# Gated layer, first chunk: SyncE issues the load of the next set's raw blocks ahead of the store of the current set's summed blocks

## The chip, the cores and the metric

The kernel runs on one core of one Trainium2 chip. The metric is the time of one execution on the device in microseconds (us); lower is better. Times of runs and times inside the profile are given apart, because the profile's span leaves out a little at both ends.

## The reference, cut to what matters

Three layers follow one another: windowed attention, a mixture of experts (one expert for each token), and a gated layer. The change is in the gated layer alone:

```python
def _moe2_ref(x, w_gate, w_val, w_out):
    gate = 1.0 / (1.0 + np.exp(-(x @ w_gate)))
    val = x @ w_val
    return (gate * val @ w_out).astype(np.float32)
```

Here x has 3072 tokens of 512 numbers, w_gate and w_val are 512 x 1536, w_out is 1536 x 512, all in float32.

## The kernel before, in words

The gated layer (class `Gated`) cuts the tokens into four chunks of 768 (`NCH` = 4, `CT` = 768). For each chunk there are two phases. The first phase computes gate and value products; it walks over twelve sets (`NSET` = 12). An even set holds a 256-column piece of w_gate and the odd set after it the same piece of w_val. The products are made with the seven-product scheme for two-by-two blocks (Strassen-Winograd): a set has four raw weight blocks and four sums of them, and seven of these eight blocks enter one product each. Every factor is split into a high and a low part, so that one product is six matmuls (two halves of 128 rows, three combinations, `product`, line 1329); a set is 42 matmuls. The second phase multiplies with w_out (`second`, line 1425).

What has to be there before a set can be multiplied, in the first chunk:

- `afetch(s)` (line 1254 in the first chunk) loads the four raw blocks of set s, 512 KB, from DRAM into a buffer named `raw`. That pool has two buffers, taken in turn, so set s+2 goes where set s was, and its load waits until all readers of set s are done.
- `asum(s)` makes the four sums with four GpSimd instructions (line 1265) into the same buffer. In its last line (1266) SyncE is told to store blocks 1 to 7, 896 KB, to the DRAM tensor `us[s]`. The three later chunks load the finished blocks from there (line 1259) and make no sums.
- `asplit(s, z)`, z = 0 and 1, turns four and then three blocks into high parts (ScalarE, line 1277) and low parts (VectorE, line 1278). These go to the tile `set`, of which there are two as well.

`first(s)` is the body of one set, written as a generator. Its order is: `asum(s+2)` in the first chunk; products X and Y; `asplit(s+1, 0)`; product Z; `asplit(s+1, 1)`; `afetch(s+3)`; now and then a load or a split of w_out blocks (`ofetch`, line 1282, at sets 3, 5, 8 and 10, 768 KB; `osplit`, lines 1287 to 1289, at sets 6 and 8, whose low part GpSimd makes and whose 1536 KB SyncE stores to `wz`); then products W, X, Z, W again, with VectorE additions between them (lines 1352, 1362, 1381, 1392, 1397, 1401). A product that uses the same accumulator a second time waits until VectorE has read the first. In odd sets GpSimd multiplies gate and value (line 1385).

The order is written out by hand. Each engine runs its own instructions strictly in that order, and so does SyncE, on which all of these loads and stores lie in one queue: a store that waits for the sums holds up the load written behind it. In program order SyncE has, for the body of set r: store of set r+2, load of set r+3, then the w_out transfers. The sets 0 to 2 are prepared in `lead(f)`, during the last eight steps of the mixture of experts: `afetch(0)` and `asum(0)` at step 4, `afetch(1)` and `asum(1)` at step 6, `afetch(2)` and the start of `first(0)` at step 7. The buffers of sets 0 and 1 are before that used by two loads of the layer's input (`yfetch`, line 1231), whose last reader is VectorE, line 1247. The input's stores `yT` come from line 1129.

Of the kernel before, what the change touches and what calls it, by code (L numbers as in the profile page):

```python
# [57 lines left out]
NSET = 2 * NJ  # L58
# [168 lines left out]
def graph():  # L227
# [12 lines left out]
    for t in range(NTILE):  # L240
# [15 lines left out]
        for s in (2 * t, 2 * t + 1):  # L256
# [4 lines left out]
            for j in range(4):  # L261
                first = [("NS", WIN if t else 128, s % 2)] if t < 2 and j == 0 else []
                add(
                    ("TTR", s, j), [("QK", s)] + first, [("QK", s, j - 2)] if j >= 2 else (),
                    cost=0.318 if i else 0.21,
                )
                add(
                    ("EXP", s, j), [("TTR", s, j)] + ([("PT", s - 3, 1)] if s >= 3 and j == 0 else []),
                    cost=0.38 if i else 0.293,
                )  # L270
# [937 lines left out]
class Gated:  # L1208
# [53 lines left out]
    def asum(self, s):  # L1262
        x = self.raw[s]
        for o, a, b, op in ((4, 0, 1, ALU.add), (6, 2, 0, ALU.subtract), (5, 4, 2, ALU.subtract), (7, 3, 5, ALU.subtract)):
            self.tc.nc.gpsimd.tensor_tensor(x[:, o, :], x[:, a, :], x[:, b, :], op=op)  # L1265
        self.tc.nc.sync.dma_start(out=self.g.us[s], in_=x[:, 1:, :].rearrange("p b n -> p (b n)"))

    def halves(self):
        return self.set_p.tile([128, 2, NJ * CH], FR, tag="set", name="set2")
# [65 lines left out]
    def first(self, s):  # L1335

        nc = self.tc.nc
        j, m = divmod(s % NSET, 2)
        V, A, G = nc.vector, nc.scalar, nc.gpsimd
        last = s % NSET == NSET - 1  # L1340
        X, Y, Z, W = (self.psum(b, f"q{b}")[:, :CH] for b in ((2, 3, 0, 1) if m else (6, 7, 4, 5)))
        u2 = self.tm.tile([128, CH], F32, tag="u2", name="u2", bufs=2)
        c, r = divmod(s, NSET)
        more = c + 1 < NCH
        if c == 0 and r < NSET - 2:
            self.asum(s + 2)
        if more and r >= NSET - 2:
            self.ysum(c + 1, r - NSET + 2)
        self.product(X, 1, 0, s)
        A.activation(u2, X, AF.Copy)  # L1350
        self.product(Y, 4, 4, s)
        V.tensor_tensor(u2, Y, u2, op=ALU.add)  # L1352
        yield
        if last:
            self.hsplit(0, 0, 2)
        else:
            self.asplit(s + 1, 0)
        self.product(Z, 5, 5, s)
        at = lambda half, tok: self.h[:, 2 * j + half, tok * CH : tok * CH + CH]
        dst = (lambda half, tok: self.g.op.tile([128, CH], F32, tag="t", name="t", bufs=3)) if m else at  # L1360
        d22 = dst(1, 1)
        V.tensor_tensor(d22, Z, u2, op=ALU.add)
        if last:
            self.hsplit(0, 2, 4)
        else:
            self.asplit(s + 1, 1)
        if r < NSET - 3:
            self.afetch(s + 3)
        elif more and r < NSET - 1:
            self.yfetch(c + 1, r - NSET + 3)  # L1370
        if c == 0:
            if r in (3, 5):
                self.ofetch((r - 3) // 2)
            if r in (6, 8):
                self.osplit((r - 6) // 2, G)
            if r in (8, 10):
                self.ofetch((r - 8) // 2 + 2)
        elif r in (2, 4, 6):
            self.oload(c, r // 2 - 1)
        self.product(W, 3, 3, s)  # L1380
        V.tensor_tensor(d22, W, d22, op=ALU.add)  # L1381

        def gate(d, half, tok):
            if m:
                (V if last else G).tensor_tensor(at(half, tok), at(half, tok), d, op=ALU.mult)  # L1385
            else:
                A.activation(d, d, AF.Sigmoid)

        gate(d22, 1, 1)
        self.product(X, 2, 1, s, False)  # L1390
        if m:
            V.tensor_tensor(at(0, 0), X, at(0, 0), op=ALU.mult)  # L1392
        else:
            A.activation(at(0, 0), X, AF.Sigmoid)
        self.product(Z, 0, 6, s, False)
        d21 = dst(1, 0)
        V.tensor_tensor(d21, Z, u2, op=ALU.add)
        gate(d21, 1, 0)
        self.product(W, 6, 2, s, False)
        d12 = dst(0, 1)  # L1400
        V.tensor_tensor(d12, W, u2, op=ALU.add)  # L1401
        gate(d12, 0, 1)
        yield
# [76 lines left out]
    def lead(self, f):  # L1480

        if f < 2:
            self.yfetch(0, f)
        if f in (1, 2):
            self.ysum(0, f - 1)
        if 2 <= f < 6:
            self.ysplit(0, f // 2 - 1, f % 2)
        if f == 3:
            sg = self.tm.tile([128, 1], F32, name="sg")
            self.tc.nc.scalar.activation(sg, self.g.nval[:, 0:1], AF.Sigmoid)  # L1490
        if f in (4, 6):
            self.afetch(f // 2 - 2)
            self.asum(f // 2 - 2)
        if f == 7:
            self.afetch(2)
            self.now = self.first(0)
            next(self.now)

# [435 lines left out]
```

## Time and profile before

| what | value |
|---|---|
| three runs | 1129.24, 1132.36, 1136.51 us; median 1132.36 us |
| the profiled execution's own time | 1134.08 us |
| its span, first to last instruction | 1132.2 us |
| mean granted TensorE clock | 0.965 of full speed |
| TensorE matmul busy | 1039.4 us, 92% of the span |
| VectorE, ScalarE, GpSimd busy | 832.5, 566.4 and 437.5 us |
| first chunk's first phase | about 545.3 to 668.5 us of the span |

How to read it: TensorE is busy nearly all the time, but matmuls are stretched when the granted clock is at its lower level, so the busy share alone doesn't show what a stage loses. A stage is read by comparing it with a stage that does the same multiplications under other conditions. Times "at 617.37" are microseconds from the start of the span.

### The profile page before, as it was taken

Reading aid. Unit: us, or ns where it says so; the run is one execution under the profiler, and the core shown is the slowest. Engines: PE = TensorE matmul, PEld = TensorE weight load, DVE = VectorE, ACT = ScalarE, POOL = GpSimd, SP = SyncE. Lnnn points to the kernel's source line nnn. Section 1 sums busy time; section 2 is a strip of 40 time slices with the busy share of each in tenths; the row PEclk is TensorE's granted clock in tenths of the full one; section 3 lists DMA queues with packets and bytes.
Section 4 is the critical chain, followed back from the end, with each engine's and each line's share of the span. In section 5 each row is a group of like instructions: output and inputs, shape, how many; then the busy total and the mean of one; then the engine's idle time right before and its main releaser. Section 6 shows DMA issues by size and latency. Waiting matters only on the chain. (4 is left out here: it accounts for less than half of the span.)

```text
span 1132.2 us, 21478 instructions
## 1 busy us (share of the span) xinstructions
PE 1039.4 (92%) x7983; PEld 990.5 (87%) x7983; DVE 832.5 (74%) x1663; ACT 566.4 (50%) x1027; POOL 437.5 (39%) x612
## 2 busy tenths in 40 slices
PE   7887878689999999999888798999999999999995
PEld 5776767679889999999777798999999999999995
DVE  6887769756678888885545689766896669866783
ACT  7997869533344445455424346344453445444440
POOL 7898778830221221213546660411503242222102
PEclk9999889798999999999989899999999999999998
DMA  9999996386698889976355658764365644656051
GB/s 188 198 179 166 187 159 146 118 189 223 200 282 274 288 281 334 305 237 192 115 179 182 246 189 299 259 235 184 110 236 190 228 167 139 247 197 243 33 213 70
DMA packets 176216, 229.45 MB, mean 203 GB/s; under 512 B 90243, under 2 KB 140038, under 8 KB 172518
## 3 DMA queue, kind: packets, MB, share of 16 engines
q1 hardware_dynamic: 170566, 214.04, 63.4%
q0 software_dynamic: 5008, 13.93, 3.5%
q8 instruction: 65, 1.06, 0.4%
q14 instruction: 49, 0.40, 0.2%
q10 hardware_dynamic: 528, 0.02, 0.0%
HBM read 163.13 MB, written 60.51 MB: 198 GB/s over the span
## 5 line engine op out<-in xcount | busy, mean ns | idle before, releaser
L1329 PE MATMUL q<-yo,set 128*128 128x384 f32 x2016 | 364.8, 342 | 20.0 <-DVE t L1381 5.9
L1329 PEld LDWEIGHTS q<-yo,set 128*128 128x128 f32 x2016 | 356.7, 192 | 27.1 <-DVE t L1381 7.5
L1425 PE MATMUL p<-wy,set 128*128 128x256 f32 x1458 | 176.5, 283 | 4.8 <-DVE set L1319 3.5
L1425 PEld LDWEIGHTS p<-wy,set 128*128 128x128 f32 x1458 | 174.9, 191 | 6.3 <-DVE set L1319 4.6
L1101 PE MATMUL hp<-xT,wh 128*128 128x256 f32 (+7 forms) x576 | 146.8, 340 | 0.1
L1385 POOL TENSOR_TENSOR h<-h,t 128x384 f32<-128x384 f32 x60 | 63.8, 1070 | 164.3 <-DVE t L1381 160.6
L1278 DVE TENSOR_TENSOR set<-raw,set 128x1024 fp32r<-128x1024 f32 x96 | 112.3, 1173 | 19.0 <-ACT set L1277 19.0
L1277 ACT ACTIVATE set<-raw 128x1024 fp32r<-128x1024 f32 x96 | 86.8, 946 | 40.0 <-POOL raw L1265 28.2
L1101 PEld LDWEIGHTS hp<-xT,wh 128*128 128x128 f32 x576 | 101.4, 191 | 3.2 <-ACT wh L999 0.4
L1101 PE MATMUL hp<-xT,wl 128*128 128x256 f32 (+7 forms) x288 | 96.5, 335 | 0.9 <-DVE wl L1004 0.9
L1118 PE MATMUL acc<-hl,wh 128*128 128x256 f32 (+7 forms) x288 | 96.3, 334 | 0.6 <-DVE hl L1106 0.5
L1118 PE MATMUL acc<-hh,wh 128*128 128x256 f32 (+7 forms) x288 | 96.5, 335 | 0.0
L1118 PE MATMUL acc<-hh,wl 128*128 128x256 f32 (+7 forms) x288 | 96.1, 334 | 0.0
L1016 POOL DMA_INDIRECT x<-xd,idx x29 | 31.5, 1085 | 159.4 <-DMA idx<-lst 138.6
L1004 DVE TENSOR_TENSOR wl<-wr,wh 128x1024 fp32r<-128x1024 f32 x64 | 80.9, 1266 | 13.9 <-ACT wh L999 13.6
L1105 ACT ACTIVATE hh<-hp 128x256 fp32r<-128x256 f32 (+7 forms) x72 | 34.7, 482 | 111.4 <-PE hp L1101 111.1
L1350 ACT ACTIVATE u<-q 128x384 f32<-128x384 f32 x48 | 23.6, 491 | 125.9 <-PE q L1329 125.9
L1352 DVE TENSOR_TENSOR u<-q,u 128x384 f32<-128x384 f32 x48 | 26.8, 558 | 78.9 <-PE q L1329 78.9
L1318 ACT ACTIVATE set<-h 128x1152 fp32r<-128x1152 f32 (+1 forms) x60 | 62.8, 1098 | 38.1 <-DVE h L1392 16.3
L1471 POOL DMA_INDIRECT out_dram<-o,idt x24 | 25.2, 1050 | 145.9 <-ACT set L1277 77.5
L561 ACT ACTIVATE pp<-tt,mall 128x232 f32<-128x232 f32 (+1 forms) x192 | 80.1, 484 | 2.4 <-DVE mall L544 2.3
L1319 DVE TENSOR_TENSOR set<-h,set 128x1152 fp32r<-128x1152 f32 (+1 forms) x60 | 77.2, 1324 | 2.0 <-ACT set L1318 1.9
(204 smaller groups left out, 2138.2 us busy)
## 6 DMA issues: line engine op xcount, KB each, us to landing
wr<-in_moe_w_dram SPq DMA_DIRECT2D x64, 512.0 KB
raw<-us SPq DMA_DIRECT2D x36, 896.0 KB
wy<-wz SPq DMA_DIRECT2D x21, 1536.0 KB
us<-raw SPq DMA_DIRECT2D x12, 896.0 KB
wz<-wy SPq DMA_DIRECT2D x7, 1536.0 KB
kn<-in_k_dram SPq DMA_DIRECT2D x24, 256.0 KB
qn<-in_q_dram SPq DMA_DIRECT2D x24, 256.0 KB
vn<-in_v_dram SPq DMA_DIRECT2D x24, 256.0 KB
```

Of the source, the lines that this page charges most:

```text
L561: nc.scalar.activation(pp[s][:, j, 256 - w :], tt[s][:, j, :w], AF.Exp, bias=g.mall[:, t, h : h + 1], scale=-1.0)
L1004: self.tc.nc.vector.tensor_tensor(lo, self.raws.pop((z, p)), hi.bitcast(F32), op=ALU.subtract)
L1101: nc.tensor.matmul(bk, a[:, k, fs], b[:, k, :], start=(m == 0), stop=(m == 11))
L1105: nc.scalar.activation(hh, bk, AF.Relu)
L1118: nc.tensor.matmul(acc[i][dk], a[:, f % 2, d], b, start=(f == 0 and m == 0), stop=(f == NF - 1 and m == 2))
L1277: self.tc.nc.scalar.activation(h, x, AF.Copy)
L1278: self.tc.nc.vector.tensor_tensor(l, x, h.bitcast(F32), op=ALU.subtract)
L1318: self.tc.nc.scalar.activation(h, x, AF.Copy)
L1319: self.tc.nc.vector.tensor_tensor(l, x, h.bitcast(F32), op=ALU.subtract)
L1329: nc.tensor.matmul(bk, w[:, za, a, us], self.y[zy][:, y, u, :], start=(start and n == 0), stop=(n == 5), skip_group_check=not start,)
L1385: (V if last else G).tensor_tensor(at(half, tok), at(half, tok), d, op=ALU.mult)
L1425: nc.tensor.matmul(bks[t], w[:, za, j, 128 * t : 128 * t + 128], y[:, zy, j, :], start=(new and j == 0 and m == 0 and (end or t != 1)), st ...
```

## The change

The store leaves `asum` and becomes a method of its own, `astore`. In the body of set r it is called behind the load of set r+3, and in `lead` the stores of sets 0 and 1 stand behind the loads of sets 1 and 2. Sums, splits, products, sizes and buffers are as before.

```diff
@@ -1263,7 +1263,9 @@
         x = self.raw[s]
         for o, a, b, op in ((4, 0, 1, ALU.add), (6, 2, 0, ALU.subtract), (5, 4, 2, ALU.subtract), (7, 3, 5, ALU.subtract)):
             self.tc.nc.gpsimd.tensor_tensor(x[:, o, :], x[:, a, :], x[:, b, :], op=op)
-        self.tc.nc.sync.dma_start(out=self.g.us[s], in_=x[:, 1:, :].rearrange("p b n -> p (b n)"))
+
+    def astore(self, s):
+        self.tc.nc.sync.dma_start(out=self.g.us[s], in_=self.raw[s][:, 1:, :].rearrange("p b n -> p (b n)"))
 
     def halves(self):
         return self.set_p.tile([128, 2, NJ * CH], FR, tag="set", name="set2")
@@ -1368,6 +1370,8 @@
             self.afetch(s + 3)
         elif more and r < NSET - 1:
             self.yfetch(c + 1, r - NSET + 3)
+        if c == 0 and r < NSET - 2:
+            self.astore(s + 2)
         if c == 0:
             if r in (3, 5):
                 self.ofetch((r - 3) // 2)
@@ -1490,9 +1494,12 @@
             self.tc.nc.scalar.activation(sg, self.g.nval[:, 0:1], AF.Sigmoid)
         if f in (4, 6):
             self.afetch(f // 2 - 2)
+            if f == 6:
+                self.astore(0)
             self.asum(f // 2 - 2)
         if f == 7:
             self.afetch(2)
+            self.astore(1)
             self.now = self.first(0)
             next(self.now)
 
```

## Rows read from the trace of the kernel before

**Rows 1.** Busy time by stretch: first phase and second phase, chunk 0 and others

```profile
core 0: us, PE busy (x) PEld busy (x) DVE busy (x) ACT busy (x) POOL busy (x), PEclk, DMA share, GB/s
...
545.30:668.50 123.20, 103.28 (x518) 96.67 (x518) 68.77 (x95) 42.67 (x65) 69.20 (x67) 0.92 0.60 206
668.50:721.45 52.95, 48.12 (x380) 46.64 (x379) 51.81 (x46) 30.11 (x30) 14.42 (x9) 0.97 0.64 240
809.10:853.80 44.70, 44.70 (x380) 44.70 (x379) 41.21 (x41) 22.90 (x25) 3.40 (x4) 1.00 0.56 202
...
853.80:941.40 87.60, 87.60 (x506) 87.42 (x506) 59.17 (x92) 37.23 (x61) 28.29 (x25) 1.00 0.52 186
```

**Rows 2.** Who waited for whom, 515 to 680: total us, times, longest

```profile
ACT set L1277 <- POOL raw L1265: 28.2, 16, 3.4
POOL raw L1265 <- DMA raw<-up: 25.8, 6, 6.2
```

**Rows 3.** SyncE queue's own waits, 535 to 665

```profile
SPq L1266 <- DMA raw<-up: 51.4, 12, 5.4
SPq L1266 <- POOL raw L1265: 47.3, 12, 7.6
...
SPq L1231 <- DMA us<-raw: 4.3, 1, 4.3
```

**Rows 4.** Chain that ended last, one set: start, us, what

```profile
617.37 0.32 SPq L1266
...
617.78 5.53 DMA raw<-up
...
623.48 2.14 POOL raw L1265 x3
...
627.32 0.86 ACT set L1277
```

**Rows 5.** SyncE in order of time: start, us of the issue, what

```profile
516.86 0.40 SPq L1129 DMA_DIRECT2D yT<-y  x1
...
521.44 1.49 SPq L1231 DMA_DIRECT2D raw<-yT  x1
...
535.78 0.37 SPq L1254 DMA_DIRECT2D raw<-up  x1
...
547.61 0.36 SPq L1254 DMA_DIRECT2D raw<-up  x1
...
557.25 0.39 SPq L1254 DMA_DIRECT2D raw<-up  x1
...
654.30 0.32 SPq L1266 DMA_DIRECT2D us<-raw  x1
...
662.13 0.33 SPq L1231 DMA_DIRECT2D raw<-yT  x1
```

**Rows 6.** Line 1266: when SyncE first passed the wait for a landed load

```profile
L1266 SPq EVENT_SEMAPHORE  x12: 17/17/17, 539.4 to 651.2; - x12
```

**Rows 7.** GpSimd in order of time: the sums of set 0, a split of w_out

```profile
541.04 6.02 POOL L1265 TENSOR_TENSOR raw<-raw 128x256 f32<-128x256 f32 x4
...
627.25 3.45 POOL L1288 TENSOR_TENSOR wy<-wr,wy 128x1536 fp32r<-128x1536 f32 x1
```

**Rows 8.** VectorE in order of time, idle before it in brackets

```profile
542.51 1.46 DVE L1247 TENSOR_TENSOR yo<-raw,yo 128x1152 fp32r<-128x1152 f32 x1
...
625.35 1.35 DVE L1278 TENSOR_TENSOR set<-raw,set 128x1024 fp32r<-128x1024 f32 x1 [1.56 <-ACT set L1277]
626.62 0.55 DVE L1362 TENSOR_TENSOR t<-q,u 128x384 f32<-128x384 f32 x1
628.20 3.32 DVE L1278 TENSOR_TENSOR set<-raw,set 128x768 fp32r<-128x768 f32 x1 [1.03 <-ACT set L1277]
```

**Rows 9.** TensorE in order of time, end of set 0 and set 1

```profile
556.74 1.31 PE L1329 MATMUL q<-yo,set 128*128 128x384 f32 x6 [1.69 <-DVE h L1362]
559.20 8.96 PE L1329 MATMUL q<-yo,set 128*128 128x384 f32 x42 [1.14 <-DVE h L1381]
```

## The prediction

> **What bounds the kernel now.** I read the stretches first. The first phase is the same work in each chunk: twelve sets of 42 matmuls. In the third chunk it takes 87.6 us, TensorE busy throughout, clock at its upper level; in the first chunk it takes 123.2 us at a mean granted clock of 0.92 [rows 1]. That is 7.30 us a set against 10.27, and 35.6 us lost in all. The first chunk's second phase loses 8.2 us as well, but there VectorE is busy for 51.81 of 52.95 us [rows 1], so the change can't reach it.
>
> Who waits for whom comes next. In the first chunk's first phase ScalarE's split waits 28.2 us for GpSimd's sums, and the sums wait 25.8 us for the load of the raw blocks [rows 2]. SyncE's own queue says why the load is late: at each of the twelve stores SyncE waits first for that set's load to land (51.4 us) and then for its sums (47.3 us) [rows 3], with the next load written behind it. The chain shows the ring for one set: store issued at 617.37, load behind it at 617.78, which takes 5.53 us, sums from 623.48, the last split at 627.32, just behind the sums [rows 4], where the next store comes. Load, sums and store follow one another without overlap: 9.95 us a set, 2.6 more than TensorE needs. The second buffer holds nothing back; the queue does.
>
> **The change part by part.** It adds and removes no instruction. Twelve stores (896 KB each) move behind one load (512 KB), or at set 9 behind the three loads of the next chunk's input. Call L(s), S(s) the issues of load and store of set s.
>
> *Removed: the wait of L for the sums.* L(s+3) now waits for the last split of set s+1 and for S(s+1) to have landed, since they read the buffer that it fills. Sums of set s+2 run beside that.
>
> *A load without a store ahead of it.* The load of set 0 had none: issued at 535.78, seen landed at 539.4, so 3.6 us [rows 5, 6], against 5.53 behind a store, or 5.94 from that store's issue [rows 4]. The 896 KB in front thus cost 5.94 − 3.6 = 2.3 us, or 2.6 us for 1 MB (estimate from these rows).
>
> *Added: the wait of L for the store.* This is the new ring: L(s+1), S(s) behind it, S(s) lands, L(s+2). No row has a store in this place. From below: both transfers took 5.94 us when the load was last. A store last costs a little more: the 736 KB store of yT issued at 516.86 let its reader go at 521.44 [rows 5], 4.6 us, where a load of that size would take 3.6 + 0.22 x 2.6 = 4.2; so 5.94 + 0.4 = 6.3. From above: the store issued at 654.30 kept the input load waiting until 662.13 [rows 3, 5], 7.8 us, with w_out transfers in front and input loads behind; with 0.4 for the load's issue, 8.2. I take 6.8, nearer to the lower row because most sets have no other transfers beside them. Some do, and lie in the same queue: two w_out loads of 768 KB (sets 3 and 5) and one store of 1536 KB (set 6) before L(11), 2.0 + 2.0 + 4.0 = 8 us by the rate above.
>
> *Start.* Both buffers are taken earlier. L(1) waits for the input's last split, which ends at 542.51 + 1.46 = 543.97 [rows 8], instead of going out at 547.61 [rows 5]. It lands at 547.6, just as the sums of set 0 end (547.06) [rows 7]. S(0) goes out then; 896 KB alone would be seen after 4.6 + 0.16 x 2.6 = 5.0 us, and the tail of L(1) adds about 0.4, so L(2) goes at 552.5 (before: 557.25 [rows 5]). Sums of set 1 end near 551.5 and are no longer late: of TensorE's stalls ahead of the last products of set 0, 1.69 + 1.14 us [rows 9], both go. Set 1 began behind one product (1.04) at 560.2; it now begins at 557.4.
>
> *The end of the phase by two limits.* TensorE's pace: 557.4 + 11 x 7.30 = 637.7. The ring: L(11) = 552.5 + 9 x 6.8 + 8 = 621.7. After it come the landing 3.6, the sums 3.8 (623.48 to 627.3 [rows 4]), the ScalarE half 0.86 [rows 4], VectorE's half 0.96 (1.35 for the larger one, so three quarters) and an addition 0.55 [rows 8], one product 1.04, set 11 itself 7.30: 18.1, so 639.8. The ring ends last by 2 us; I take 639.8.
>
> *Cover that goes.* The load no longer keeps the sums away from the splits, so GpSimd and VectorE meet more. What a meeting can cost: a three-block split took 3.32 us at 628.20, ending after GpSimd's 3.45 us split of w_out from 627.25 [rows 7, 8], 2.4 over the 0.96. Two such GpSimd instructions lie in this phase; one falls into a split by the times above (set 8: after the sums of set 10), the other mostly before one. I add 2.4 for it, and about 1 for sums against splits, since a 1.35 us split beside running sums [rows 4, 8] is at most a tenth over its size. The end is 643.2.
>
> *The rest.* SyncE's load of the next input at set 9 moves ahead of one store, both more than 20 us before they are used. Nothing in the second phase reads `us`. The clock: in the third chunk, with TensorE never idle, it is at the upper level throughout [rows 1]; the lower level in the first chunk went with its stalls, and the 7.30 us contain that return already.
>
> **Sum.** 668.5 − 643.2 = 25.3 us off the profiled execution's 1134.08: 1108.8. That execution lies 1.7 above the median 1132.36; against the median the result is 1107.1.
>
> **One rule weighed.** Beside running sums the split at 625.35 took 1.35 us [rows 4, 8], hardly more than usual. The Trainium skill, SBUF — State Buffer, "Who interferes with whom", says of a VectorE instruction with two SBUF inputs and a GpSimd instruction that whichever starts first holds the shared ports for its whole length and the other blocks. The 3.32 us row agrees. By that rule each split could be held up by one sum, which is the second rival below.
>
> **Rivals.**
>
> *The store ring is slower.* At 8.2 us a set, the upper row, L(11) = 552.5 + 73.8 + 8 = 634.3, the end 652.4 + 2.4, gain 13.7: 1118.7 by the median. For it: the row at 654.30; against it: that store had over 2 MB ahead of it.
>
> *Sums and splits block each other.* In TensorE's pace the sums of a set fall just into the splits of the set before. A sum takes 2.14 / 3 = 0.71 us [rows 4]; two splits held up by one each make 1.4 us a set, of which I estimate half a us is covered by the time that VectorE has left (59.17 busy of 87.6 us [rows 1] leaves 2.4 a set, but most of it lies behind the splits). So 0.9 x 11 = 10, and both w_out splits 4.8: the end 637.7 + 14.8 = 652.5, gain 16: 1116.4. For it: the 3.32 us row; against it: the 1.35 us row.
>
> *TensorE's pace with nothing lost.* The end is 637.7, gain 30.8: 1101.6. This is the most that there is.
>
> *Slower than before.* The store now waits behind a load that itself waits for a split and an earlier store. If a store behind a load is seen landed only after more than 9.5 us, the new ring is longer than the old 9.95. With 11 us a set, L(11) = 552.5 + 99 + 8 = 659.5, the end 677.6: 9 slower, 1141.5. No row comes near: the longest is 7.8 us.
>
> *No effect.* If the sums were released by something besides the load (GpSimd's multiplications in odd sets lie ahead of them), loads would land early and wait. Then only the start's 2.8 us and little more goes: 1128. Against it: the 25.8 us that the sums wait for the load [rows 2].
>
> **How the numbers follow.** Forecast (1103 to 1113) 0.62; slower ring 0.14; blocked splits 0.13; TensorE's pace alone 0.05; no effect 0.03; slower 0.03. The predicted time is the forecast's, 1107. The range reaches from just under TensorE's pace to a little over the two middle rivals: 1101 to 1120. About 1% is what a measurement of this kernel tells from no change, so faster means below 1121: the forecast, TensorE's pace and nearly all of the two middle rivals, 0.91; within 1% takes what is left of them and no effect, 0.06; slower 0.03.
>
> **What would show it.** In the profile after: the first phase of chunk 0 in about 98 us instead of 123.2; loads issued directly behind the last split instead of behind a store, landing in about 3.6 us; the sums' wait for the load nearly gone; SyncE's wait for the load at line 1266 gone, and a wait of the load for the store of two sets before (about 6.4 us behind that store's issue) in its place; the first chunk's second phase at 53 us as before. Wrong would be: a load still 5.5 us long; stores that take over 7.8 us; splits lengthened to 2 us throughout; a clock of 0.92 again with TensorE seldom idle; a second phase that gives the gain back.

## The result, and the profile after

The changed kernel takes 1103.22 us (median of 4 runs, 1098.23 to 1105.9) against 1132.93 us for the kernel before (4 runs): a ratio of 0.9744, 95% interval 0.9716 to 0.9771, so 29.7 us faster. The forecast was 1107, with 1101 to 1120 as its range. The profiled execution took 1103.0 us, with a span of 1101.1.

The stretches first, as in [rows 1]: the first chunk's first phase, its second phase, and for the start of the program the attention's last score matmuls (line 532).

```profile
core 0: us, PE busy (x) PEld busy (x) DVE busy (x) ACT busy (x) POOL busy (x), PEclk, DMA share, GB/s
539.82:635.18 95.36, 92.69 (x519) 88.64 (x518) 66.02 (x95) 41.00 (x66) 74.43 (x68) 1.00 0.75 263
...
635.20:687.00 51.80, 46.81 (x380) 45.20 (x379) 50.65 (x45) 29.97 (x30) 12.30 (x7) 1.00 0.66 250
```

The first phase takes 95.36 us instead of 123.2, and it says how: TensorE's idle time falls from 123.2 − 103.28 = 19.9 to 2.7 us, and its busy time from 103.28 to 92.69. The granted clock is at its upper level (2.4 GHz) throughout instead of 0.92 on average. Before, it was at the lower level (1.2 GHz, a granted clock of 0.50) in four stretches of the phase; the first begins inside the stalls of [rows 9]. The first of them, and the sum of the four:

```profile
558.84:562.26 3.42, 3.06 (x10) 3.06 (x11) 1.32 (x3) 1.46 (x4) 0.00 (x0) 0.50 0.91 277
...
sum 20.50, PE 17.76 PEld 17.26 DVE 8.00 ACT 5.43 POOL 8.54; mean PE 4.44 PEld 4.31 DVE 2.00 ACT 1.36 POOL 2.13
```

So 17.2 us are waits that are gone. Of the 10.6 us of busy time, about 9 (an estimate: half of the 17.76 us busy at half clock) are matmuls no longer stretched by the lower level; where the other 1.7 come from isn't shown. The second phase, 51.8 us, is about 1 us shorter.

That makes about 29 us, while the spans differ by 31.1. The rest lies where the change isn't. In the profile before the first phase begins at 545.30, here at 539.82, and the difference is there already at the end of the attention, where the instructions are the same; this is line 532 before, and then after:

```profile
L532 PE MATMUL s<-kT,qt x576: 213/259/398, 10.2 to 211.1; 64*128 64x232 f16 x160, 64*128 64x128 f16 x32
```

```profile
L532 PE MATMUL s<-kT,qt x576: 213/259/398, 10.4 to 204.8; 64*128 64x232 f16 x160, 64*128 64x128 f16 x32
```

The last score matmul starts at 211.1 in one and at 204.8 in the other. In the profiles of the experiments below it starts between 204.0 and 212.7, with the attention's instructions unchanged: this varies from one execution to the next. On the other side the profile after loses 3.2 us behind 687, mostly after its last matmul. The lengths of the first phase are therefore the sharper measure below, from its first matmul of line 1329 (1331 after the change) to the first of the second phase.

SyncE's own waits, against [rows 3]:

```profile
SPq L1254 <- DMA us<-raw: 43.0, 10, 5.8
SPq L1268 <- POOL raw L1265: 11.5, 10, 2.6
...
SPq L1254 <- DVE set L1280: 4.8, 5, 1.7
```

The store (now line 1268) no longer waits for its own set's load (51.4 us before), and for the sums 11.5 us instead of 47.3. In place of that the load waits for the store of two sets before, ten times, 43 us in all. It is a long wait on a queue, and it costs next to nothing, as the waits of the computing engines show, against [rows 2]:

```profile
POOL raw L1265 <- DMA raw<-up: 5.7, 4, 2.5
...
ACT set L1279 <- POOL raw L1265: 3.4, 2, 2.9
```

The sums wait 5.7 us for loads (25.8 before), and ScalarE 3.4 us for the sums (28.2 before). One set in SyncE's order of time, against the four rows of [rows 4]:

```profile
558.71 0.36 SPq L1254 DMA_DIRECT2D raw<-up  x1
560.21 0.33 SPq L1268 DMA_DIRECT2D us<-raw  x1
565.64 0.36 SPq L1254 DMA_DIRECT2D raw<-up  x1
```

The load goes out 1.5 us ahead of the store; the store is seen landed 5.4 us after its issue, and the next load follows: 6.93 us for the ring. The chain through the same stretch is nearly all TensorE:

```profile
546.76 14.77 PE q L1331 x84
...
581.53 29.66 PE q L1331 x168
...
619.28 16.06 PE q L1331 x90
```

Here 168 matmuls, four sets, take 29.66 us with nothing else on the chain.

### The profile page after: what moved, and what is told of

It is laid out like the page before. It is cut to its first block, busy times and chain, and to the rows that moved or that the text cites. A ratio compares the mean times of both kernels' runs of the same rounds, so it can differ in the third digit from the quotient of the medians.

```text
span 1101.1 us, 21478 instructions
## 1 busy us (share of the span) xinstructions
PE 1028.4 (93%) x7983; PEld 981.2 (89%) x7983; DVE 829.0 (75%) x1663; ACT 566.3 (51%) x1027; POOL 441.5 (40%) x612
## 4 chain that ended last, share of the span: by engine, by line
PE 71%; POOL 10%; DVE 6%; DMA 5%; issue 4%; ACT 2%; SPq 1%; another core or an unknown queue 0%; POOLq 0%; DVEq 0%; ACTq 0%
PE q L1331 30%; PE p L1429 14%; PE hp L1101 12%; PE acc L1118 12%; DMA vb<-vv 2%; POOL pl L597 1%; POOL xr L640 1%; PE mxt L1036 1%; POOL vv L484 1%; POOL lst L735 1%; DMA wr<-in_moe_w_dram 1%; DVE set L1321 1%; POOL ph L590 1%; DMA x<-xd,idx 1%; PE ptp L573 1%
## 5 line engine op out<-in xcount | busy, mean ns | idle before, releaser
L1331 PE MATMUL q<-yo,set 128*128 128x384 f32 x2016 | 354.5, 337 | 3.1 <-ACT set L1279 1.3
L1331 PEld LDWEIGHTS q<-yo,set 128*128 128x128 f32 x2016 | 348.6, 188 | 8.0 <-DVE h L1385 2.3
L1389 POOL TENSOR_TENSOR h<-h,t 128x384 f32<-128x384 f32 x60 | 60.6, 1018 | 164.2 <-DVE t L1385 160.6
L1004 DVE TENSOR_TENSOR wl<-wr,wh 128x1024 fp32r<-128x1024 f32 x64 | 80.9, 1266 | 13.2 <-ACT wh L999 11.8
```

Source lines behind the costliest of these rows:

```text
L1004: self.tc.nc.vector.tensor_tensor(lo, self.raws.pop((z, p)), hi.bitcast(F32), op=ALU.subtract)
L1331: nc.tensor.matmul(bk, w[:, za, a, us], self.y[zy][:, y, u, :], start=(start and n == 0), stop=(n == 5), skip_group_check=not start,)
```

## The experiments

All times are medians. The kernel before, run beside them, took 1132.20 us in the first four, 1132.66 in the next three and 1129.27 in the last two.

**One half of the change at a time.** First the start alone:

```diff
             self.asum(s + 2)
+            self.astore(s + 2)
...
-        if c == 0 and r < NSET - 2:
-            self.astore(s + 2)
```

> Only the stores of sets 0 and 1 stand behind the next load; in the body of a set the store is ahead of the load again, as before. Theory (a ring of load, sums and store in SyncE's queue sets the pace of the first phase): the ring starts some 4.7 us earlier (its load of set 2 at 552.5 instead of 557.25 by the trace of before) and then runs at the old 9.9 us a set, so the time is 1126 to 1130 us, 3 to 6 below before. Rival (the start is what holds the phase, and the body only follows): most of the change's 29 us is there already, 1103 to 1110 us.

Measured: 1125.12 us, ratio 0.9942 (0.9918 to 0.9965), and a first phase of 116.0 us (542.98 to 659.02). The body keeps its old pace:

```profile
608.01 0.32 SPq L1268 DMA_DIRECT2D us<-raw  x1
608.42 0.39 SPq L1254 DMA_DIRECT2D raw<-up  x1
617.95 0.32 SPq L1268 DMA_DIRECT2D us<-raw  x1
```

9.94 us from store to store, the step that [rows 4] begin with. The rival falls. The gain of 7.1 us is a little over the 3 to 6 expected: the load of set 2 goes out at 548.40, 5.4 us after the phase begins, where I had reckoned 7.2 (552.5 − 545.3), and the kernel before had 11.95 (557.25, [rows 5], less 545.30): 6.5 earlier, not 4.7.

Then the body alone:

```diff
             self.afetch(f // 2 - 2)
-            if f == 6:
-                self.astore(0)
             self.asum(f // 2 - 2)
+            self.astore(f // 2 - 2)
         if f == 7:
             self.afetch(2)
-            self.astore(1)
```

> Only the body of a set has the load ahead of the store; the stores of sets 0 and 1 are ahead of the next load, as before. Theory (the ring of the body): TensorE's pace from set 1 on, which starts 2.8 us later than with the whole change, so 1105 to 1108 us, about 3 above the whole change. Rival (the start): little is gained, 1125 us or more.

Measured: 1109.36 us, ratio 0.9823 (0.9793 to 0.9852), first phase 99.8 us. That is 1.4 us over the range given, but on the side of the theory: 23.3 of the 27.8 us are in the body. The late start costs 4.5 us against the whole change: TensorE is idle 5.8 us instead of 2.7, and busy 94.1 instead of 92.7 at a mean granted clock of 0.98.

**Was it the wait, or the transfer ahead of the load?** Moving the store does two things: SyncE no longer waits for the sums before it issues the load, and the load's data no longer lie behind 896 KB. This kernel keeps the wait and moves the data:

```diff
     def astore(self, s):
-        self.tc.nc.sync.dma_start(out=self.g.us[s], in_=self.raw[s][:, 1:, :].rearrange("p b n -> p (b n)"))
+        x = self.raw[s][:, 1:, :].rearrange("p b n -> p (b n)")
+        self.tc.nc.sync.dma_start(out=self.g.us[s][:, : 13 * 128], in_=x[:, : 13 * 128])
+
+    def apart(self, s):
+        x = self.raw[s][:, 1:, :].rearrange("p b n -> p (b n)")
+        self.tc.nc.sync.dma_start(out=self.g.us[s][:, 13 * 128 :], in_=x[:, 13 * 128 :])
...
             self.asum(s + 2)
+            self.apart(s + 2)
...
             self.asum(f // 2 - 2)
+            self.apart(f // 2 - 2)
```

> The whole change, but the last 128 columns (64 KB) of the 1792 are stored in a piece of their own ahead of the next load; the other 832 KB stay behind it. SyncE thus waits for the sums before each load again, while nearly nothing is transferred ahead of the load. Theory (the wait in the queue costs): the ring is load 3.7 + sums 4 + issues and hops 0.8 = 8.5 us a set, so the first phase takes about 109 us and the time is 1114 to 1121 us; the load takes 3.6 to 4 us and SyncE waits for it and for the sums again. Rival (the transfer of 896 KB ahead of the load was all that cost, not the wait): 1102 to 1106 us, as with the whole change.

Measured: 1123.53 us, ratio 0.9914 (0.9879 to 0.995), first phase 112.9 us. SyncE's order of time and its waits:

```profile
602.07 0.32 SPq L1273 DMA_DIRECT2D us<-raw  x1
602.49 0.38 SPq L1254 DMA_DIRECT2D raw<-up  x1
602.92 0.46 SPq L1269 DMA_DIRECT2D us<-raw  x1
610.82 0.32 SPq L1273 DMA_DIRECT2D us<-raw  x1
```

```profile
SPq L1273 <- POOL raw L1265: 85.6, 12, 10.9
```

A set takes 8.75 us (8.5 expected); SyncE waits 85.6 us for the sums ahead of its loads. The rival, that the transfer was all, falls; the time is 2.5 us above the upper end that I gave. Of the 27.8 us this kernel gains 10.3 (123.1 to 112.9), and the other 17.5 go only when the wait goes as well. That is no clean division, because the load isn't free of the store here. The first row is from this kernel, the second from the whole change:

```profile
606.97 3.81 POOL L1265 TENSOR_TENSOR raw<-raw 128x256 f32<-128x256 f32 x4 [4.93 <-DMA raw<-up]
```

```profile
569.37 4.53 POOL L1265 TENSOR_TENSOR raw<-raw 128x256 f32<-128x256 f32 x4 [1.65 <-DMA raw<-up]
```

The sums start 4.5 us after their load's issue (602.49), with the 832 KB issued 0.4 us behind it. In the whole change, where the store follows 2.1 us behind (565.64 and 567.75), it is 3.7 us, and in the kernel before it was 5.7 (617.78 to 623.48, [rows 4]). The 0.8 us between 4.5 and 3.7 make some 8 us over ten sets (an estimate), which belong to the transfer. So the transfer's place is worth 10 us or more and the wait 17.5 or less; which is the larger isn't settled.

**How near is the new ring?** Each store once more, behind the first:

```diff
     def astore(self, s):
         self.tc.nc.sync.dma_start(out=self.g.us[s], in_=self.raw[s][:, 1:, :].rearrange("p b n -> p (b n)"))
+        self.tc.nc.sync.dma_start(out=self.g.ut[s], in_=self.raw[s][:, 1:, :].rearrange("p b n -> p (b n)"))
...
```

> The whole change, with each store of a set made a second time into another DRAM tensor (another 896 KB a set, behind the first). Theory (the new ring, load to store to load, lies only little under TensorE's pace): another 2.3 us in the ring, 6.8 to about 9 a set, so that it ends last: the phase grows by 12 to 18 us and the time is 1115 to 1122 us. Rival (the stores have plenty of room, TensorE alone sets the pace): within 2 us of the whole change, 1102 to 1106 us.

Measured: 1122.80 us, ratio 0.9928 (0.9902 to 0.9954), first phase 110.9 us, 15.5 more than the whole change; the time is 0.8 us above the range given. The loads follow each other like this:

```profile
552.51 0.37 SPq L1254 DMA_DIRECT2D raw<-up  x1
...
561.81 0.37 SPq L1254 DMA_DIRECT2D raw<-up  x1
...
635.53 0.37 SPq L1254 DMA_DIRECT2D raw<-up  x1
```

Nine steps from 552.51 to 635.53, 9.2 us each: now the ring ends last. Less one store (896 KB x 2.6 us a MB, 2.3) that is 6.9 for the ring with one store, the 6.8 of the prediction. TensorE's 7.30 lies only 0.4 above it. The same doubling in the kernel before, where the second store lies ahead of the load as well:

```diff
         self.tc.nc.sync.dma_start(out=self.g.us[s], in_=x[:, 1:, :].rearrange("p b n -> p (b n)"))
+        self.tc.nc.sync.dma_start(out=self.g.ut[s], in_=x[:, 1:, :].rearrange("p b n -> p (b n)"))
...
```

> The kernel before, with each store of a set made a second time into another DRAM tensor, ahead of the next load as the first one is. Theory (in the old order each transfer ahead of the load lies in the ring with its whole length): 2.3 us and an issue of 0.4 more for each of some 11 sets, so 1156 to 1164 us. Rival (the load's 5.5 us had another cause than the store ahead of it): less than 10 us more, below 1142 us.

Measured: 1158.42 us, ratio 1.022 (1.0168 to 1.0272), first phase 147.9 us, 24.7 more: 2.25 us for each of eleven sets, close to the 2.3 that I reckoned for 896 KB. In the old order a transfer ahead of the load lies in the ring with its whole length.

**The changed kernel again,** without an edit, for what varies:

> The changed kernel as it is, once more, for the runs beside it and for what varies between executions. Theory (the change acts in the first chunk alone): the first phase of chunk 0 takes 95 to 96 us again, while the attention stage before it, whose instructions are those of before, differs by some us from one profiled execution to another; the ratio to before is 0.972 to 0.978. Rival (the earlier end of the attention stage, some 6 us in the first profile, is an effect of the change): the attention stage ends near 205 us again, and not near 211.

Measured: 1103.53 us, ratio 0.9734 (0.9695 to 0.9772), first phase 95.3 us. The last score matmul starts at 208.1, between the two values above. With the old order (the doubled store in the kernel before) it starts at 208.0, with the sums' wait kept at 212.7. The rival, which had it near 205 again, isn't borne out. The profiles alone don't exclude a smaller effect: where the body's loads wait for the sums it starts at 208.0 to 212.7 (four profiles), elsewhere at 204.0 to 208.5 (seven). The medians leave little room for one: 29.7, 29.1 and, below, 28.2 us in three comparisons, against some 29 us in the two phases that the change reaches.

**What the phase still loses.** TensorE's pace from the prediction gives 12.1 + 80.3 = 92.4 us; the phase takes 95.4. TensorE's weight loads wait for VectorE's two additions, which lie behind the splits:

```profile
PEld q L1331 <- DVE h L1385: 1.8, 6, 0.4
PEld q L1331 <- DVE t L1385: 0.8, 2, 0.4
PEld q L1331 <- DVE t L1364: 0.5, 1, 0.5
PEld q L1331 <- DVE h L1364: 0.4, 1, 0.4
```

In this profile, set by set, these waits follow the length of the larger split in front of them: 0 to 0.2 us behind splits of 1.2 to 1.5 us, 0.2 to 0.4 behind 1.6 to 1.8, 0.8 to 0.9 behind the two of 2.1 and 2.2. Two experiments ask why. In the first VectorE makes the sums of sets 2 to 11, at the end of a set, so that GpSimd's can't meet the splits:

```diff
-        if c == 0 and r < NSET - 2:
-            self.asum(s + 2)
...
-        if c == 0 and r < NSET - 2:
-            self.astore(s + 2)
...
         V.tensor_tensor(d12, W, u2, op=ALU.add)
         gate(d12, 0, 1)
+        if c == 0 and r < NSET - 2:
+            self.asum(s + 2, V)
+            self.astore(s + 2)
         yield
```

> The whole change, with the sums of sets 2 to 11 made by VectorE at the end of a set's body instead of by GpSimd at its start, and their store behind them. Theory (what the phase still loses against TensorE's pace, about 3 us, comes from splits that meet GpSimd's sums): the larger split goes from 1.6 back to 1.2 us, the phase takes 92.5 to 94 us, and the time is 1 to 3 us below the whole change run beside it. Rival (VectorE has too little time left: 1.3 to 1.5 us more a set): additions that TensorE waits for come later, the phase takes 97 us or more and the time is 1 to 8 us above the whole change.

Measured: 1105.23 us beside 1103.53 for the whole change, a difference that lies inside the spread of either (1102.18 to 1107.42 and 1101.28 to 1105.86), and a first phase of 97.2 us. VectorE's groups in the phase, mean time behind the comma:

```profile
L1265 DVE TENSOR_TENSOR raw<-raw 128x256 f32<-128x256 f32 x40 | 21.3, 571 | 0.3
L1280 DVE TENSOR_TENSOR set<-raw,set 128x1024 fp32r<-128x1024 f32 x12 | 15.1, 1261 | 0.4 <-ACT set L1279 0.4
```

and the larger split of the whole change in the run beside it:

```profile
L1280 DVE TENSOR_TENSOR set<-raw,set 128x1024 fp32r<-128x1024 f32 x12 | 18.8, 1566 | 0.4 <-ACT set L1279 0.4
```

The split does go back from 1.57 to 1.26 us when GpSimd makes no sums beside it. The phase's number is the rival's, but most of the excess has another reason. These are the start of the phase and the rest of it, from the last five products of set 0 on, with VectorE's sums and then in the whole change beside it:

```profile
538.67:546.84 8.17, 6.11 (x27) 5.24 (x26) 3.23 (x5) 1.97 (x4) 5.25 (x6) 0.79 0.64 203
546.84:635.89 89.05, 88.95 (x493) 85.33 (x493) 77.55 (x130) 40.38 (x63) 27.55 (x20) 1.00 0.69 249
```

```profile
540.21:547.07 6.86, 4.70 (x26) 3.86 (x25) 3.29 (x5) 1.97 (x4) 5.25 (x6) 1.00 0.66 213
547.07:635.48 88.41, 87.89 (x495) 85.51 (x493) 62.02 (x90) 39.35 (x63) 69.32 (x62) 1.00 0.75 268
```

Of the 1.95 us more, 1.3 lie in the start, before VectorE makes its first sum (at 552.90); there the granted clock is 0.79 on average, after stalls like those at which it stayed at 1.00 in the whole change. The rest takes 0.6 us longer. So shorter splits win nothing: the sums take 0.57 us each on VectorE, 2.4 us a set behind the odd sets, where GpSimd's multiplications run, and the next set's first addition is late. Neither forecast is shown.

In the second, the later of the two additions goes ahead of the smaller split:

```diff
+        if c == 0 and not last:
+            self.product(W, 3, 3, s)
+            V.tensor_tensor(d22, W, d22, op=ALU.add)
         if last:
             self.hsplit(0, 2, 4)
         else:
             self.asplit(s + 1, 1)
...
-        self.product(W, 3, 3, s)
-        V.tensor_tensor(d22, W, d22, op=ALU.add)
+        if c or last:
+            self.product(W, 3, 3, s)
+            V.tensor_tensor(d22, W, d22, op=ALU.add)
```

> The whole change, and in the first chunk VectorE's second addition of a set (of product W, whose accumulator TensorE uses again) stands ahead of the smaller split of the next set instead of behind it; the load of the next raw blocks moves with that split. Theory (the 3 us that the first phase is over TensorE's pace are stalls of some 0.4 us a set, because this addition stands behind two splits of which the larger is lengthened to 1.6 to 2.2 us): the stalls behind this addition go, those behind the first addition (two sets) stay, the phase takes 92.5 to 94 us instead of 95.4, and the time is 1 to 3 us below the whole change. Rival (the loads go out 0.5 us later and the ring, which has little room, ends last instead): the phase stays at 95 us or grows, and GpSimd's sums wait longer for their loads.

> The changed kernel as it is, beside the run above on the same chip: 1101 to 1106 us, a first phase of 95 to 96 us.

Measured: 1101.10 us beside 1101.05, first phases of 94.6 us both (538.11 to 632.70 and 541.24 to 635.86). The waits of the weight loads with the addition ahead:

```profile
PEld q L1331 <- DVE t L1364: 1.5, 2, 0.9
...
PEld q L1331 <- DVE h L1364: 0.7, 3, 0.3
```

The waits for the later addition are gone, as the theory said, but the first addition, behind the lengthened larger split, now holds TensorE for 2.2 us. Nothing is won: whichever addition stands behind the larger split takes up the delay. These 2.2 us are also what the phase lies over 92.4.

## Why the prediction was right, step by step

*What bounds the phase: right.* The ring of load, sums and store in SyncE's queue set the pace; doubling the store lengthened it by a store's time for each set, and keeping only the wait kept 8.75 us a set.

*A load without a store ahead of it: right in size.* 3.6 us was taken. In the profile after, the load of set 1 goes out at 538.5 and the sums that wait for it start at 542.27, 3.8 us later. That this part gives 10.3 us or more, and the wait's removal 17.5 or less, is from the experiment that kept the wait.

*The new ring: right in size, 6.8 against 6.9.* The 6.9 are the doubled stores less one. The single ring of 6.93 read above lies in a phase that TensorE paces, so it says less. But the ring's place in the sum was wrong by two terms. The ring was to end last by 2 us (639.8 against TensorE's 637.7). It didn't: L(11) goes out at 611.08, 65.8 us after L(2), 7.3 a set as TensorE takes, where the forecast had 9 x 6.8 + 8 = 69.2. The 8 us for w_out transfers is the term that was too large. The steps from load to load with such a transfer take 7.70, 7.54 and 7.99 us, the six others 6.64 to 7.70. With the doubled stores, where the ring does end last, the three take 8.99, 9.52 and 8.82, the others 8.78 to 10.13, and all nine lie only 4.0 us over nine of the shortest. And L(2) goes 5.4 us after the phase's start instead of 7.2: the store of set 0, issued while the last of L(1) was still landing, let its buffer go 3.6 us after its issue, where the forecast had 5.0 + 0.4 = 5.4.

*The start: right.* Both stalls of [rows 9] are gone; 546.60 plus five products of 1.04 is 551.8, 12.0 us after the phase's start, where the forecast had 12.1.

*Cover that goes: the mechanism right, both sizes wrong, and close only by luck.* Sums and splits do meet more. Before, the larger split beside sums took 1.32 to 1.36 us in eight of the twelve sets, like the 1.35 of [rows 8]; after, seven of the last eleven take 1.5 to 2.2. The means are alike, 1.64 and 1.63, because one split before took 3.65. The first row is from the third chunk before, without sums, the second one such split after:

```profile
L1278 DVE TENSOR_TENSOR set<-raw,set 128x1024 fp32r<-128x1024 f32 x11 | 13.4, 1216 | 0.0
```

```profile
570.11 1.79 DVE L1280 TENSOR_TENSOR set<-raw,set 128x1024 fp32r<-128x1024 f32 x1
```

I added about 1 us for this, from the row of 1.35. And I added 2.4 us for a w_out split that falls into a split. It fell where the prediction put it, after the sums of set 10:

```profile
615.17 2.18 DVE L1280 TENSOR_TENSOR set<-raw,set 128x1024 fp32r<-128x1024 f32 x1
```

The split took 2.18 instead of 1.2, 1.0 more and not 2.4; GpSimd's instruction (612.75 to 616.27) had 1.1 us left when it began. The weight loads behind it wait 0.9 us (0.48 and 0.42), of 3.5 us in the phase. So the meeting with w_out costs 0.9 us or less where 2.4 stood, and the sums have the rest, some 2.6, where 1 stood. All of this together costs TensorE 3.0 us over its pace, where the forecast had 2.1 + 3.4 = 5.5. Hence 27.8 us in this phase instead of 25.3, and one more in the second phase, which the prediction left out and no run explains.

*The rivals.* Blocked splits, at a full sum each, would have taken the phase to 107 us (652.5 − 545.3); it took 95. The slower ring needed 8.2 us a set; it takes 6.9. That the load was hidden anyway would have left GpSimd's waits where they were. TensorE's pace with nothing lost, given 0.05, was nearer to the measured time than the forecast.

## What to carry to other kernels

A queue that issues in order turns a store that waits for a result into a wait of every load behind it: put the load whose buffer comes free first, and the store behind it. Then count the ring that the new order makes, here load, store, the same buffer's next load, 6.9 us against a pace of 7.3: doubling one transfer shows how much room it has. And read the granted clock with the stalls, since some 9 of these 27.8 us were matmuls that ran at the lower level after waits.

## What was not expected

The store of set 0, 896 KB in rows of 7 KB, let its buffer go 3.6 us after its issue, as soon as a load of 512 KB lands; the 736 KB store of yT from which the prediction started took 4.6. Their rows, their targets and what lay in the queue behind them differ; which of these counts wasn't tried.

The end of the attention moves between 204.0 and 212.7 us from one execution to another with the same instructions. Two profiles can therefore differ by nearly 9 us ahead of any stage that an edit to the gated layer touches, and they should be compared by the lengths of the stage.
